# A new order of the work up to block 8, and the keys' maximum spread by a transpose, in a fused attention, feed-forward and soft-MoE kernel

## Chip, cores and metric

The kernel runs on one core of a Trainium2 chip. The metric is the time of one execution on the device, in microseconds (us). The engines' names are those of the profile: PE is TensorE with its matmuls, PEld its loading of weights, DVE VectorE, ACT ScalarE, POOL GpSimd, SP SyncE, which here only issues transfers.

## The reference

Three layers follow each other: a linear attention, a gated feed-forward layer, and a soft mixture of experts.

```python
# attention: B, H, S, D = 8, 8, 576, 64
q_s = exp(q - max(q, -1));  q_s = q_s / (sum(q_s, -1) + 1e-9)
k_s = exp(k - max(k, 2));   k_s = k_s / (sum(k_s, 2) + 1e-9)      # along the sequence
kv  = einsum('bhsd,bhse->bhde', k_s, v)
x   = einsum('bhsd,bhde->bhse', q_s, kv)      # then laid out as x[4608, 512]
# feed-forward: 512 -> 1536 -> 512
x = (silu(x @ w_gate) * (x @ w_val)) @ w_out
# soft MoE: 8 experts with 4 slots each, phi[512, 32], w1[8, 512, 1024], w2[8, 1024, 512]
logits = x @ phi
d = softmax(logits, 0);  slot_input = d.T @ x
slot_out[e] = relu(slot_input[e] @ w1[e]) @ w2[e]
out = softmax(logits, 1) @ slot_out
```

## The kernel before

**Tiles and blocks.** The 4608 tokens are worked on in ten blocks, numbers 0 to 7 of 512 tokens and 8 and 9 of 256. Each array of float64 weights comes in as pairs of 32-bit integers and is made float32 by ACT, DVE and POOL (`cv_a`, `cv_b`, `cv_c`, L513 to L540).

**Attention.** `load_kn`, `load_vn` and `load_q` (L287 to L313) fetch keys, values and queries of one batch (or block) and part. For the keys, `k_max` (L318) takes the maximum over five of a partition's elements on DVE, transposes the 128x128 result on PE (`kpT`, L323) and takes the maximum again on DVE. That leaves one maximum for each of 128 channels, a column of 128x1. `k_exp` (L329) spreads it along the other axis on PE (`kmbp`, L331), subtracts it on DVE and applies the exponential on ACT. `kv` (L340) multiplies keys and values on tiles of 128x32 of the array, 20 small products in all, and DVE and ACT normalise the result into `kvs`. The queries go through `q_a` and `q_b` (L370 to L419). Their transpose `qT` (L442) runs on PE for blocks 0 and 1 and on DVE from block 2 on. `x_mul` (L455) multiplies queries by `kvs` on tiles of 64x64 (`px`, L485). ACT copies `px` to the high half `x` (L495), and DVE subtracts to get the low half (L497).

**Feed-forward.** `pair(n, i)` makes the hidden tile `hT` number i of twelve in block n: a run of twelve products on the full array for the gate (`g`, L595), a run of twelve for the value (`v`, L595), then silu on ACT (L602), a product on DVE (L604). Twelve are four k tiles by three products of halves (weights' high by x high and low, weights' low by x high). The tile of the weights that belongs to i is `W[i]`; its high half is a copy on ACT (L553), its low half a subtraction on DVE. In blocks 0 and 1 each hT goes to memory by a DMA on SP (`hT_dr`, L608), from a pool of six buffers; from block 2 on DVE transposes it (`hB`, L615) and a DMA lays it out anew (L635). In the last blocks PE does that (`hNp`, L641).

**Soft MoE.** `lg` (L661) multiplies hT by `wp`, which is the output weights times phi, on tiles of 128x32. `post_a` to `post_d` form the softmax pieces, and `dh` (L784) gathers the slots' inputs, again on 128x32. After the last block the experts' weights come in 64 pieces (`piece`, L818, on POOL), and the experts and the output follow.

**What sets the order.** All stages are generators. A table of text, `PROGRAM` (L49), lists 2301 steps such as `kexp 0 1` or `pair 3 7`, and each entry moves its generator to its next `yield` (L1109 to L1115). So each engine has its instructions in the order of the table, and nothing else orders them; waits between engines come from what reads and writes what. An entry with `@` makes a POOL instruction wait for a DVE instruction named behind it. The line of k_exp that the change touches is the matmul in

```python
mx, mb = kmax.pop((b, p)), misc((128, 128), "kmbp")
nc.tensor.matmul(mb, lhsT=mx.to_broadcast([128, 128]), rhs=ident, start=True, stop=True)
yield
```

A column repeated 128 times is multiplied by the identity; in the trace this takes two instructions on PE, the transpose `kpT` of the same shape takes one. PSUM tiles for `kpT`, `kmbp`, `kv`, `qT` and `px` come from a pool of three (`misc`), for g and v from two each.

Of the kernel before, what the change touches and what calls it, by code (L numbers as in the profile page):

```python
# [39 lines left out]
def rows(n):  # L40
# [19 lines left out]
    pair 0 0, qb 1 1, wb 1, wb 1, wh 2, pair 0 0, qb 1 1, wb 4, wa 4 2, wl 2 v, wh 3, wb 4, pair 0 2, wa 6 4, wl 3 v,  # L60
    qt 1 0, kmax 1 0, wc 1@wl 3 v, wa 7 5, kmax 1 0, pair 0 2, pair 0 2, kmax 1 1, kmax 1 0, qa 1 2, wh 1, wb 4,
    pair 0 3, pair 0 0, wl 1 v, qb 1 1, pair 0 2, wc 4@wl 1 v, pair 0 0, pair 0 1, pair 0 2, wa 6 4, pair 0 0, wa 5 3,
    wb 6, wb 6, wh 4, kmax 1 1, kexp 1 0, pair 0 1, wb 6, pair 0 1, kexp 1 0, wc 6@wb 6, wa 5 3, kmax 1 1, kexp 1 0,
    pair 0 3, pair 0 1, pair 0 1, wl 4 v, qb 1 2, wb 5, kexp 1 1, kv 1 0, wb 7, qt 1 1, kexp 1 1, kn 1 2, vn 1 3,
    pair 0 4, wh 6, kv 1 0, q 1 3, wb 7, kexp 1 1, wl 6 v, wa 7 5, const rep, wb 5, pair 0 4, kv 1 0, pair 0 4, wb 5,
    kmax 1 2, wc 5@wb 5, pair 0 3, kv 1 1, pair 0 4, qt 1 1, kmax 1 2, pair 0 6, kn 1 3, wa 8 4, pair 0 3, pair 0 4,
    wb 7, vn 1 2, wh 5, pair 0 3, qb 1 2, wa 8 4, wl 5 v, pair 0 6, qb 1 2, wb 8, w 10 1, wb 8, kmax 1 3, wc 7@wb 8,
    pair 0 6, pair 0 5, kv 1 1, kmax 1 2, kv 1 1, pair 0 6, pair 0 6, qa 1 3, wh 7, pair 0 5, wb 8, pair 0 5, qb 1 3,
    wl 7 v, wc 8@wl 7 v, kmax 1 3, kexp 1 2, pair 0 7, pair 0 5, kexp 1 2, pair 0 5, kmax 1 3, wa 9 5, qb 1 3,
    pair 0 7, wh 8, wb 9, wb 9, kexp 1 2, wl 8 v, wa 9 5, kexp 1 3, kv 1 2, wa 10 4, kexp 1 3, pair 0 8, vn 2 0, wb 9,  # L70
    kn 2 1, wa 10 4, kv 1 2, wc 9@wb 9, kexp 1 3, kv 1 2, kv 1 3, pair 0 7, pair 0 8, kv 1 3, wb 10, vn 2 1, w 11 0,
    kn 2 0, wh 9, wb 10, wb 10, kv 1 3, qb 1 3, x 1 0, wl 9 v, pair 0 7, wc 10@wl 9 v, pair 0 8, pair 0 9, x 1 0,
    pair 0 7, pair 0 8, x 1 0, pair 0 8, x 1 0, wh 10, o 1, x 1 0, pair 0 9, pair 0 9, wl 10 v, wa 11 5, kmax 2 0,
    wa 11 5, wb 11, x 1 1, wb 11, wb 11, qt 1 2, x 1 1, pair 0 10, qt 1 2, q 2 1, x 1 1, pair 0 9, wc 11@wb 11, x 1 1,
    x 1 1, pair 0 9, x 1 2, wh 11, o 0, qt 1 3, x 1 2, pair 0 10, wl 11 v, pair 0 10, q 2 3, qt 1 3, qa 2 1, oa 1,
    x 1 2, qa 2 1@wl 11 v, oa 1, x 1 3, pair 0 10, ob 1, pair 0 10, x 1 2, pair 0 11, qa 2 1, x 1 2, qa 2 1@qa 2 1,
    oa 0, ob 1, x 1 3, qb 2 1, x 1 3, pair 0 11, ob 1, ob 0, x 1 3, pair 0 11, x 1 3, oc 1@ob 0, qb 2 1, pair 1 1,
    qa 2 3, oa 0, pair 0 11, qa 2 3, o 3, pair 0 11, ob 0, pair 1 3, ob 0, qa 2 3, oc 0@qa 2 3, pair 1 1, pair 1 1,
    qb 2 1, o 2, qa 2 3, pair 1 0, pair 1 1, qb 2 1, pair 1 1, qb 2 3, qb 2 1@qb 2 1, pair 1 0, qt 2 1, pair 1 0,
    qb 2 3, q 2 0, qb 2 3, pair 1 3, pair 1 3, qb 2 3, pair 1 0, qb 2 3@qb 2 3, pair 1 0, kmax 2 0, op 0, pair 1 3,  # L80
    pair 1 2, oa 2, qa 2 0, pair 1 3, op 0, qa 2 0, oa 2, kmax 2 0, kmax 2 1, ob 2, pair 1 6, ob 2, ob 2, qa 2 0,
    oc 2@qa 2 0, pair 1 2, pair 1 2, qa 2 0, o 4, pair 1 9, pair 1 2, qb 2 0, pair 1 2, qb 2 0, pair 1 9, pair 1 9,
    qb 2 0, qb 2 0, qb 2 0@qb 2 0, kexp 2 0, kmax 2 1, pair 1 4, pair 1 9, kmax 2 1, pair 1 9, qt 2 0, kexp 2 0,
    q 2 2, kexp 2 0, pair 1 6, pair 1 6, pair 1 4, pair 1 4, pair 1 6, qa 2 2, pair 1 6, qa 2 2, pair 1 11, pair 1 4,
    pair 1 4, qa 2 2, qa 2 2@qa 2 2, qb 2 2, kexp 2 1, kv 2 0, kexp 2 1, pair 1 11, vn 2 2, kv 2 0, kn 2 3, kexp 2 1,
    qb 2 2, kv 2 0, qb 2 2, pair 1 11, kv 2 1, qb 2 2, pair 1 10, kv 2 1, vn 2 3, pair 1 11, kv 2 1, kn 2 2,
    qb 2 2@qb 2 2, pair 1 11, kmax 2 3, pair 1 5, kmax 2 3, op 0, op 1, kmax 2 3, op 0, kmax 2 2, kexp 2 3, pair 1 5,
    pair 1 5, kexp 2 3, oa 3, op 1, oa 3, ob 3, ob 3, pair 1 7, kexp 2 3, ob 3, pair 1 5, oc 3@ob 3, pair 1 5,
    kmax 2 2, x 2 0, kmax 2 2, kexp 2 2, pair 1 7, pair 1 7, qt 2 2, o 5, kexp 2 2, q 3 0, qt 2 3, kexp 2 2, q 3 1,
    pair 1 8, pair 1 7, pair 1 7, x 2 0, x 2 0, x 2 0, x 2 0, kv 2 2, kv 2 3, kv 2 2, vn 3 2, kv 2 2, pair 1 8,  # L90
    kn 3 2, pair 1 8, kv 2 3, vn 3 0, qa 3 0, kn 3 0, qa 3 1, qa 3 0, kv 2 3, qa 3 1, x 2 1, pair 1 8, qa 3 0,
    pair 1 8, qa 3 1, op 3, qa 3 0@qa 3 1, x 2 1, pair 1 10, pair 1 10, x 2 1, qa 3 1, x 2 1, kmax 3 2, oa 5, x 2 1,
    qb 3 0, ob 5, pair 2 2, u 0, pair 1 10, ob 5, pair 1 10, oa 5, qb 3 0, qb 3 0@ob 5, pair 2 2, qb 3 1, pair 2 2,
    qb 3 1, qb 3 0, ob 5, op 2, pair 2 2, qb 3 1@ob 5, ua 0, op 1, pair 2 6, op 2, oc 5, op 1, oa 4, oa 4, pair 2 3,
    ob 4, ua 0, qb 3 1, ob 4, ob 4, kmax 3 2, op 2, pair 2 3, pair 2 3, kmax 3 2, qb 3 1@ob 4, op 2, op 3, kmax 3 0,
    oc 4, qt 3 1, pair 2 1, pair 2 3, qb 3 0, ub 0, q 3 3, ub 0, pair 2 1, pair 2 1, ub 0, qt 3 0, uc 0@ub 0,
    pair 2 0, pair 2 1, qa 3 3, q 3 2, ud 0, u 1, qa 3 3, pair 2 0, pair 2 0, qa 3 3, qa 3 3@qa 3 3, qb 3 3, pair 2 4,
    pair 2 0, pair 2 0, pair 2 1, qa 3 2, pair 2 4, pair 2 2, pair 2 4, qa 3 2, qb 3 3, qa 3 2, qb 3 3@qa 3 2, ua 1,
    pair 2 6, qa 3 2, pair 2 4, ua 1, ub 1, ub 1, pair 2 6, ub 1, qb 3 2, pair 2 5, pair 2 6, uc 1, qb 3 2, op 3,
# [1087 lines left out]
```

## Time and profile before

| | before |
|---|---|
| median of three runs | 838.16 us (838.03 to 841.31) |
| profiled execution | 836.75 us, span 835.0 us, 1.75 us around the span |
| mean granted clock of TensorE | 0.99 of full speed |
| PE, DVE, ACT, POOL busy | 789.7, 466.3, 389.3, 259.5 us |
| read and written in HBM | 105.22 MB and 25.17 MB |

The page sums up one profiled execution. Its first part gives busy time by engine, its second part cuts the span into 40 slices of 20.9 us, its fifth part groups instructions by line. Start times of single instructions come from timelines of one engine. A timeline's bar ends where the hardware's pipeline is modelled to end, and so bars of neighbouring products overlap: the distance between two starts says how long the engine was held.

### The profile page before, as it was taken

The numbers are of one execution on the slowest core, as the hardware profiler recorded it, in microseconds if no ns is written. First come the engines' busy times: TensorE is split into PE (matmuls) and PEld (weight loads), VectorE is DVE, ScalarE is ACT, GpSimd is POOL, SyncE is SP. The second block draws the span as 40 slices with busy tenths as digits, with TensorE's granted clock in tenths as the row PEclk, the third lists the DMA queues.
The fourth block names the chain that finished last, engine by engine and source line by source line (L and its number), as shares of the span: only waits on it lengthen the run. The fifth ranks groups of instructions, "written<-read, shape, count | busy, mean of one in ns | idle before, by whom it ended". The sixth has DMA issues, their size and how long they took to land.

```text
span 835.0 us, 15748 instructions
## 1 busy us (share of the span) xinstructions
PE 789.7 (95%) x6045; PEld 603.7 (72%) x6045; DVE 466.3 (56%) x1016; ACT 389.3 (47%) x628; POOL 259.5 (31%) x505
## 2 busy tenths in 40 slices
...
GB/s 346 411 73 177 203 173 143 126 158 96 97 89 158 128 173 160 162 146 183 125 146 141 87 180 183 188 38 117 129 99 105 54 70 296 269 366 392 408 287 355
DMA packets 103243, 151.10 MB, mean 181 GB/s; under 512 B 60032, under 2 KB 73728, under 8 KB 99200
## 3 DMA queue, kind: packets, MB, share of 16 engines
...
q14 instruction: 27, 0.22, 0.1%
HBM read 105.22 MB, written 25.17 MB: 156 GB/s over the span
## 4 chain that ended last, share of the span: by engine, by line
PE 81%; DMA 10%; SPq 3%; DVE 2%; issue 1%; ACT 1%; POOL 0%; DVEq 0%; POOLq 0%
PE v L595 33%; PE g L595 32%; DMA piece<-in_w_dram 3%; PE dh L784 3%; SPq L635 3%; PE lg L661 3%; PE kv L346 2%; PE px L485 2%; DMA f<-in_wgv_dram 2%; DMA vn<-in_vn_dram 1%; PE o L1060 1%; DMA kn<-in_kn_dram 1%; DMA wo<-wo_st 1%; DMA h0T<-hT_dr 1%; PE kmbp L331 1%
## 5 line engine op out<-in xcount | busy, mean ns | idle before, releaser
L595 PE MATMUL g<-x,W 128*128 128x512 f32 (+1 forms) x1440 | 319.5, 373 | 0.0
L595 PE MATMUL v<-x,W 128*128 128x512 f32 (+1 forms) x1440 | 316.7, 371 | 0.0
L595 PEld LDWEIGHTS g<-x,W 128*128 128x128 f32 x1440 | 250.0, 189 | 53.5 <-issue 7.8
L595 PEld LDWEIGHTS v<-x,W 128*128 128x128 f32 x1440 | 249.6, 189 | 51.6 <-issue 7.2
L604 DVE TENSOR_TENSOR hT<-hT,v 128x512 f32<-128x512 f32 (+1 forms) x120 | 75.6, 633 | 162.9 <-PE v L595 126.7
L602 ACT ACTIVATE hT<-g 128x512 f32<-128x512 f32 (+1 forms) x120 | 65.4, 555 | 169.2 <-PE g L595 128.4
L363 POOL COPY qsd<-qsd 32x16 f32<-32x16 f32 (+1 forms) x256 | 52.3, 204 | 111.6 <-DVE qsd L386 61.8
L368 POOL TENSOR_TENSOR qd<-qd,qsd 128x512 f32<-128x512 f32 (+1 forms) x64 | 59.5, 939 | 43.0 <-DVE qsd L390 10.0
L602 ACT ACT_TABLE_LOAD x52 | 66.7, 1283 | 9.5 <-PE g L595 4.0
L615 DVE STREAM_TRANSPOSE hB<-hT 128x512 f32<-128x512 f32 (+1 forms) x78 | 49.8, 670 | 7.7 <-DMA hN<-hB 6.5
L818 POOL DMA_DIRECT2D piece<-in_w_dram x54 | 28.5, 530 | 45.5 <-PE v L595 24.1
L338 ACT ACTIVATE kn<-kn 128x640 f32<-128x640 f32 x32 | 23.4, 737 | 33.9 <-DVE kn L334 31.6
L300 POOL DMA_DIRECT2D vn<-in_vn_dram x24 | 13.5, 562 | 81.1 <-PE kv L346 81.1
...
L495 ACT ACTIVATE x<-px 128x512 fp32r<-128x512 f32 (+1 forms) x44 | 21.2, 514 | 33.8 <-PE px L485 33.7
L540 POOL TENSOR_TENSOR ost<-ost,f 128x1024 int32<-128x1024 int32 x9 | 21.9, 2435 | 38.6 <-DVE W L557 11.7
L334 DVE TENSOR_TENSOR kn<-kn,kmbp 128x640 f32<-128x640 f32 x32 | 25.6, 809 | 13.2 <-PE kmbp L331 13.0
L346 PEld LDWEIGHTS kv<-vn,kn 128*32 128x32 f32 x1280 | 24.5, 149 | 10.2 <-issue 7.0
L419 ACT ACTIVATE qd<-qd 128x512 f32<-128x512 f32 (+1 forms) x32 | 18.0, 576 | 25.7 <-POOL qd L368 25.6
L346 PE MATMUL kv<-vn,kn 128*32 128x65 f32 x1280 | 27.6, 239 | 1.5 <-DMA vn<-in_vn_dram 1.4
L497 DVE TENSOR_TENSOR x<-px,x 128x512 fp32r<-128x512 f32 (+1 forms) x44 | 24.5, 584 | 7.4 <-ACT x L495 7.2
L320 DVE TENSOR_REDUCE kpart<-kn 128x128 f32<-128x640 f32 x32 | 25.9, 808 | 4.9 <-PE kpT L323 2.5
...
## 6 DMA issues: line engine op xcount, KB each, us to landing
...
f<-in_wgv_dram SPq DMA_DIRECT2D x9, 1024.0 KB, 11.0
...
out_dram<-ob SPq DMA_DIRECT2D x7, 1024.0 KB, 10.4
hT_dr<-hT SPq DMA_DIRECT2D x24, 256.0 KB, 3.1
ost<-in_woT_dram SPq DMA_DIRECT2D x6, 1024.0 KB, 6.7
```

What stands on the lines that cost most here:

```text
L320: nc.vector.tensor_reduce(out=part, in_=kn_t[b, p], axis=AX, op=ALU.max)
L334: nc.vector.tensor_tensor(out=t, in0=t, in1=mb.unsqueeze(2).to_broadcast([128, 128, ST]), op=ALU.subtract)
L346: nc.tensor.matmul(acc[r:r + 32, :], lhsT=ek[:, r:r + 32, i], rhs=vv[:, i, r // D, :], start=(i == 0), stop=(i == ST - 1), tile_position=( ...
L363: nc.gpsimd.tensor_copy(out=st[a:a + 32, o + 1], in_=st[b:b + 32, o])
L368: nc.gpsimd.tensor_tensor(out=a, in0=a, in1=s, op=op)
L595: nc.tensor.matmul(gv[j], lhsT=W[i][:, w, k, j, :], rhs=x[:, k, :], start=(k == 0 and w == 0 and x is xh), stop=(k == KT - 1 and w == 1),)
L602: nc.scalar.activation(out=s, in_=g, func=ACTF.Silu)
L604: nc.vector.tensor_tensor(out=s, in0=s, in1=v, op=ALU.mult)
L615: nc.vector.transpose(out=hB[n, i // w][:, :, i % w, :], in_=s.rearrange("p (b j) -> p b j", j=32))
L635: nc.sync.dma_start(out=hN[n][32 * b:32 * b + 32, :, a, w * g:w * g + w, :], in_=src[:, :, b])
L661: nc.tensor.matmul(lg[n][32 * g:32 * g + 32, :], lhsT=wp[:, i, :], rhs=hs[:, g] if n < NSP else hs[g], start=(r == 0), stop=(r == end), ti ...
L818: nc.gpsimd.dma_start(out=ap, in_=src)
```

## The change

Two things change. In `k_exp` the matmul with the identity becomes a transpose of the same repeated column:

```diff
     def k_exp(b, p):
         mx, mb = kmax.pop((b, p)), misc((128, 128), "kmbp")
-        nc.tensor.matmul(mb, lhsT=mx.to_broadcast([128, 128]), rhs=ident, start=True, stop=True)
+        nc.tensor.transpose(mb, mx.to_broadcast([128, 128]), ident)
         yield
 PROGRAM = """
-    q 0 0, q 0 1, const ident, kn 0 1, q 0 3, kn 0 0, w 0, kn 0 2, kn 0 3, q 0 2, w 2, qa 0 0, w 3, w 1, qa 0 1,
+    q 0 0, kn 0 1, qa 0 0, kmax 0 1, q 0 3, qa 0 0, qb 0 0, q 0 1, const ident, qa 0 3, qa 0 1, kmax 0 1, kmax 0 1,
...
```

And the table has the same 2301 steps in another order. The last 396 steps, from the first pieces of the experts' weights on, stand as before. Three places show what the new order does. A row of these listings is a line of code, the instruction, what it writes and reads, its tile, and how often it stands in a row.

PE from the fourth `kmbp` (before) or the third (after) to the first feed-forward product. Before:

```order
L331 MATMUL kmbp<-ident,kmax 128x128
L346 MATMUL kv<-vn_132,kn 32x65 x20
L346 MATMUL kv<-vn,kn 32x65 x20
L346 MATMUL kv<-vn_132,kn_106 32x65 x40
L442 MATMUL qT<-ident,q_95 128x128 x4
L485 MATMUL px<-qsT_184,kvs_91 64x128 x32
L442 MATMUL qT<-ident,q 128x128 x4
L595 MATMUL g<-x_380,W 128x512
```

And now:

```order
L331 MATMUL kmbp<-ident,kmax 128x128
L346 MATMUL kv<-vn_189,kn 32x65 x20
L331 MATMUL kmbp<-ident,kmax 128x128
L346 MATMUL kv<-vn_189,kn_129 32x65 x20
L346 MATMUL kv<-vn,kn 32x65 x20
L346 MATMUL kv<-vn_189,kn_129 32x65 x20
L442 MATMUL qT<-ident,q_95 128x128 x4
L485 MATMUL px<-qsT_155,kvs_91 64x128 x32
L595 MATMUL g<-x_353,W 128x512
```

The second `qT`, which is of block 1, moved behind the first feed-forward product, and the first `kv` moved ahead of the last `kmbp`. On SP, the loads at the start before (`f` are weights as integers, `vn` the values):

```order
L313 DMA q_95<-in_q_dram 128x512
L510 DMA f_110<-in_wgv_dram 128x2048
L510 DMA f_114<-in_wgv_dram 128x2048
L510 DMA f_116<-in_wgv_dram 128x2048
L313 DMA q<-in_q_dram 128x512
L300 DMA vn<-in_vn_dram 128x650
L313 DMA q<-in_q_dram 128x512
L300 DMA vn_132<-in_vn_dram 128x650 x2
L300 DMA vn<-in_vn_dram 128x650
L300 DMA vn_132<-in_vn_dram 128x650
```

And now:

```order
L313 DMA q_95<-in_q_dram 128x512
L510 DMA f_141<-in_wgv_dram 128x2048
L510 DMA f_143<-in_wgv_dram 128x2048
L300 DMA vn_189<-in_vn_dram 128x650
L313 DMA q<-in_q_dram 128x512
L300 DMA vn_189<-in_vn_dram 128x650 x2
L300 DMA vn<-in_vn_dram 128x650
L510 DMA f_243<-in_wgv_dram 128x2048
```

One weight load moved from ahead of the first block's four `vn` to behind them. In the middle, PE around the `kv` and `px` of block 3, before:

```order
L595 MATMUL g<-x_1718,W 128x512
L595 MATMUL g<-x_1717,W 128x512
L485 MATMUL px<-qsT,kvs_91 64x192 x4
L485 MATMUL px<-qsT,kvs_92 64x320 x4
L346 MATMUL kv<-vn,kn 32x65 x20
L661 MATMUL lg<-hT,wp 32x512 x4
L595 MATMUL v<-x_1717,W 128x512
L595 MATMUL v<-x_1718,W 128x512
```

And now:

```order
L595 MATMUL g<-x_1652,W 128x512
L595 MATMUL g<-x_1651,W 128x512
L346 MATMUL kv<-vn,kn 32x65 x40
L661 MATMUL lg<-hT,wp 32x512 x4
L485 MATMUL px<-qsT,kvs_91 64x192 x4
L485 MATMUL px<-qsT,kvs_92 64x320 x4
L595 MATMUL v<-x_1651,W 128x512
L595 MATMUL v<-x_1652,W 128x512
```

Two `kv`, an `lg` and a `px` now stand together between two runs on the full array, where one of the two `kv` stood elsewhere before. Last, SP's writes of hT in block 0 and 1, between loads of weights (`ost` are the output weights as integers), before:

```order
L510 DMA ost<-in_woT_dram 128x2048
L608 DMA hT_dr<-hT 128x512
L510 DMA ost<-in_woT_dram 128x2048
L608 DMA hT_dr<-hT 128x512
L510 DMA ost<-in_woT_dram 128x2048
L608 DMA hT_dr<-hT 128x512
L510 DMA ost<-in_woT_dram 128x2048
L608 DMA hT_dr<-hT 128x512 x3
L510 DMA ost<-in_woT_dram 128x2048
L608 DMA hT_dr<-hT 128x512 x6
```

And now:

```order
L510 DMA ost<-in_wgv_dram 128x2048 x2
L608 DMA hT_dr<-hT 128x512 x2
L912 DMA phi_sb<-in_phi_dram 128x128
L510 DMA ost<-in_woT_dram 128x2048 x2
L608 DMA hT_dr<-hT 128x512 x4
L510 DMA ost<-in_woT_dram 128x2048 x2
L608 DMA hT_dr<-hT 128x512 x6
L510 DMA ost<-in_woT_dram 128x2048
L608 DMA hT_dr<-hT 128x512 x3
```

Loads that stood one by one now stand in twos, and more writes stand in a row behind them.

## Rows read from the trace of the kernel before

**Rows 1.** Page, parts 1 and 2: busy us (share), instructions; GB/s in 40 slices.

```profile
PE 789.7 (95%) x6045; PEld 603.7 (72%) x6045; DVE 466.3 (56%) x1016; ACT 389.3 (47%) x628; POOL 259.5 (31%) x505
...
GB/s 346 411 73 177 203 173 143 126 158 96 97 89 158 128 173 160 162 146 183 125 146 141 87 180 183 188 38 117 129 99 105 54 70 296 269 366 392 408 287 355
```

**Rows 2.** Windows: stretch, length, busy us of PE PEld DVE ACT POOL, clock, DMA, GB/s.

```profile
40.00:60.00 20.00, 19.84 (x89) 15.72 (x88) 18.06 (x24) 19.94 (x42) 7.50 (x4) 1.00 0.25 97
650.00:700.00 50.00, 49.36 (x327) 41.02 (x329) 28.48 (x70) 20.41 (x31) 14.30 (x39) 1.00 0.41 100
800.00:835.00 35.00, 15.93 (x168) 8.58 (x160) 11.67 (x22) 11.59 (x25) 0.00 (x0) 0.80 0.75 304
```

**Rows 3.** Timeline of PE, middle: start us, length us, instructions [idle before <-releaser].

```profile
293.69 0.38 PE L331 MATMUL kmbp<-ident,kmax 128*128 128x128 f32 x2
293.83 3.01 PE L595 MATMUL v<-x,W 128*128 128x512 f32 x12
296.77 0.86 PE L346 MATMUL kv<-vn,kn 128*32 128x65 f32 x40
...
309.78 3.01 PE L595 MATMUL g<-x,W 128*128 128x512 f32 x12
312.72 1.06 PE L661 MATMUL lg<-hT,wp 128*32 128x512 f32 x8
313.71 0.49 PE L331 MATMUL kmbp<-ident,kmax 128*128 128x128 f32 x2
...
477.20 1.04 PE L661 MATMUL lg<-h0T,wp 128*32 128x512 f32 x8
478.06 1.04 PE L661 MATMUL lg<-hT,wp 128*32 128x512 f32 x8
...
486.66 2.88 PE L595 MATMUL v<-x,W 128*128 128x512 f32 x12
489.38 0.27 PE L323 MATMUL kpT<-ident,kpart 128*128 128x128 f32 x1
489.41 3.00 PE L595 MATMUL g<-x,W 128*128 128x512 f32 x12
492.25 2.88 PE L595 MATMUL v<-x,W 128*128 128x512 f32 x12
```

**Rows 4.** Timeline of PE, the start and the first hNp of block 8.

```profile
23.96 4.89 PE L346 MATMUL kv<-vn,kn 128*32 128x65 f32 x160 [1.43 <-DMA vn<-in_vn_dram]
28.78 0.83 PE L442 MATMUL qT<-ident,q 128*128 128x128 f32 x4
...
35.23 0.81 PE L442 MATMUL qT<-ident,q 128*128 128x128 f32 x2 [2.76 <-ACT q L413]
...
36.79 4.22 PE L595 MATMUL g<-x,W 128*128 128x512 f32 x12
...
707.76 0.60 PE L641 MATMUL hNp<-ident,hT 128*128 128x128 f32 x4
```

**Rows 5.** Chain of waits, start of the span: start us, length us, what.

```profile
12.70 11.12 DMA vn<-in_vn_dram
```

**Rows 6.** Timeline of ACT, columns as for PE: copy and conversion of weights.

```profile
26.00 1.05 ACT L553 ACTIVATE W<-ost 128x1024 fp32r<-128x1024 f32 x1
...
38.12 1.18 ACT L518 ACTIVATE ost<-f 128x1024 f32<-128x1024 f32 x1
```

**Rows 7.** Page, part 6: DMA issues, count, KB each, median us to landing.

```profile
f<-in_wgv_dram SPq DMA_DIRECT2D x9, 1024.0 KB, 11.0
...
hT_dr<-hT SPq DMA_DIRECT2D x24, 256.0 KB, 3.1
```

**Rows 8.** Timeline of POOL: two pieces of the experts' weights.

```profile
718.04 1.08 POOL L818 DMA_DIRECT2D piece<-in_w_dram  x2 [6.96 <-PE v L595]
```

**Rows 9.** Page, part 5: line, group, count, busy us, mean ns, idle before.

```profile
L602 ACT ACT_TABLE_LOAD x52 | 66.7, 1283 | 9.5 <-PE g L595 4.0
...
L602 ACT ACTIVATE hT<-g 128x512 f32<-128x512 f32 (+1 forms) x120 | 65.4, 555 | 169.2 <-PE g L595 128.4
```

More of the change, by code (lines that the diff above doesn't have):

```diff
@@ L60 @@
[L60 to L99, printed above, removed]
@@ new lines @@
+    x 2 0, x 2 0, kexp 2 2, kexp 2 2, pair 1 4, qa 2 2@qa 2 2, qb 2 2, qb 2 2, qb 2 2, o 5, pair 1 7, qb 2 3,
+    pair 1 7, x 2 0, x 2 0, qb 2 3@qb 2 3, pair 1 6, kexp 2 3, qb 2 2, qt 2 3, pair 1 11, pair 1 7, pair 1 7,
+    kexp 2 2, pair 1 7, x 2 0, pair 1 10, qb 2 2@qb 2 2, pair 1 6, kv 2 2, qt 2 2, pair 1 6, vn 2 3, q 3 0, kv 2 2,
+    pair 1 0, kv 2 3, op 3, q 3 1, kv 2 3, kn 3 0, qa 3 1, vn 3 0, kv 2 2, op 1, op 1, pair 1 10, pair 1 10, qa 3 1,
+    qa 3 0, qa 3 1, oa 5, kv 2 3, x 2 1, x 2 1, pair 1 10, pair 1 8, x 2 1, ob 5, op 2, x 2 1, qa 3 0, qa 3 0, x 2 1,
@@ new lines @@
+    ub 1, ub 1, ub 1, kn 3 1, qb 3 2, qb 3 2, pair 2 4, pair 2 7, kmax 3 1, kmax 3 1, pair 2 8, kmax 3 1, kexp 3 1,
+    kv 3 0, kexp 3 1, vn 3 3, uc 1, pair 2 8, kexp 3 3, kexp 3 3, pair 2 5, pair 2 9, qb 3 3, pair 2 7, qb 3 2,
+    kv 3 2, kexp 3 1, sh 2 0, sh 2 0, qb 3 2, kexp 3 3, kv 3 1, kv 3 3, ud 1, sh 2 1, sh 2 1, pair 2 7, lg 2 1,
+    kv 3 1, vn 4 1, kv 3 1, x 3 0, x 3 0, pair 2 8, x 3 0, qb 3 2, pair 2 9, qb 3 3, qt 3 3, pair 2 11, q 4 2,
+    pair 2 11, pair 2 9, pair 2 9, qt 3 2, sh 2 1, x 3 0, kv 3 3, kv 3 3, qa 4 2, x 3 1, x 3 1, x 3 0, vn 4 0, op 5,
@@ new lines @@
+    pair 2 10, pair 2 10, x 3 1, x 3 1, kn 4 0, pair 2 11, pair 2 11, op 5, q 4 0, sh 2 1, qa 4 2, qa 4 2, pair 2 11,
+    pair 2 10, x 3 1, kn 4 3, kmax 4 0, pair 3 3, qa 4 0, pair 2 9, qa 4 0, qa 4 0, qa 4 0, qb 4 0, pair 2 10,
+    pair 2 10, pair 3 3, u 2, pair 2 7, ua 2, sh 2 3, pair 2 8, lg 2 2, kmax 4 0, pair 3 6, pair 2 6, pair 3 6,
+    qb 4 0, pa 2, qb 4 0, kmax 4 0, kmax 4 3, ub 2, ua 2, ub 2, kexp 4 0, ub 2, kmax 4 3, pa 2, pb 2, sh 2 3,
+    pair 3 3, qb 4 0, pair 3 3, sh 2 2, pair 3 0, pair 3 6, pair 3 0, kmax 4 3, kexp 4 0, kexp 4 0, pb 2, pair 3 0,
@@ new lines @@
+    pair 3 10, pair 3 5, uc 2, sh 2 2, qa 4 2, pb 2, kv 4 0, ud 2, pair 3 6, kexp 4 3, lt 0 0, pair 3 5, qb 4 0,
+    qt 4 0, q 4 1, ts 0 0, qa 4 1, pair 3 5, pair 3 0, sh 2 3, sh 2 3, ts 0 0, sh 2 2, ts 0 0, kn 4 1, qa 4 1, qa 4 1,
+    qa 4 1, qb 4 1, pb 2, pb 2, kv 4 0, ts 0 0, pair 3 1, pair 3 1, pair 3 1, pair 3 1, qb 4 2, pair 3 1, pair 3 2,
+    sh 2 2, qb 4 1, pair 3 2, kexp 4 3, qb 4 1, qb 4 1, kmax 4 1, pair 3 2, qb 4 2, pair 3 2, ts 0 0, kmax 4 1,
+    kmax 4 1, pair 3 7, vn 4 3, qb 4 1, ts 0 0, kexp 4 1, lg 3 0, lg 0 0, kexp 4 1, kexp 4 1, qb 4 2, qt 4 1,
@@ new lines @@
+    pair 3 8, pair 3 8, kexp 4 2, kexp 4 2, pair 3 7, sh 3 1, pair 3 11, q 5 0, qb 4 3, qt 4 3, kexp 4 2, kv 4 2,
+    kv 4 3, lg 3 1, pair 3 8, pair 3 6, sh 3 1, kv 4 2, kn 5 1, kv 4 2, kv 4 3, kv 4 3, sh 3 2, q 5 1, x 4 1, qa 5 0,
+    x 4 1, x 4 1, x 4 1, sh 3 2, x 4 1, qa 5 0, pair 3 11, pd 2, vn 5 1, pair 3 9, qa 5 0, pair 3 9, kmax 5 1,
+    kmax 5 1, qa 5 0, vn 5 0, pair 4 5, kn 5 0, kmax 5 1, qb 5 0, lt 0 2, pair 3 11, kexp 5 1, qa 5 1, kexp 5 1,
+    pair 3 9, qa 5 1, pair 4 5, qa 5 1, sh 3 2, kmax 5 0, pair 4 4, qb 5 0, sh 3 2, qa 5 1, pair 3 9, pair 4 4,
@@ new lines @@
+    sh 3 3, q 5 3, pair 4 1, pd 2, pb 3, qa 5 3, qa 5 3, pair 4 1, pair 4 1, pb 3, pb 3, sh 3 3, qa 5 3, pb 0, pb 3,
+    pair 4 10, pb 3, pair 4 2, pair 4 2, pair 4 4, sh 3 3, qa 5 3, pb 3, ln 0 0, pair 4 10, pair 4 6, pair 4 2,
+    pair 4 2, kv 5 0, kv 5 0, pair 4 0, ln 0 1, pc 3, pb 0, pc 0, pc 0, pair 4 1, vn 5 2, pd 2, lg 4 0, kmax 5 2,
+    kv 5 0, kn 5 3, vn 5 3, kmax 5 2, pair 4 6, pair 4 6, pair 4 6, kmax 5 3, qb 5 3, qb 5 3, qb 5 3, pair 4 7,
+    kmax 5 2, pair 4 7, kmax 5 3, qa 5 2, sh 4 0, pair 4 7, qb 5 3, ln 0 3, ln 0 2, pair 4 7, pc 0, pc 0, qb 5 2,
```

274 lines of the change are left out of this document (142 added, 132 removed).

## Prediction

> **What bounds the kernel now.** I read the page first: TensorE (PE) is busy for 789.7 of 835.0 us [rows 1]. Then the stretches: from 40 to 760 us PE has almost no idle time; three stretches of 50 us lose 0.34 to 0.64 us each, together 1.5 us, and the last of them stands for the three [rows 2]. The rest of the 45 us of idle time lies before the first feed-forward product at 36.79 us [rows 4] and in the last 75 us, where the experts' weights and the output stream [rows 2]. So the middle is a sum of PE's work, and what an edit there is worth is read from where the next PE row *starts*, not from the length of a bar. Last I read the timeline of PE: a run of twelve products on the full array takes 2.72 us from its start to the start of what follows (486.66 to 489.38 [rows 3]); around products on tiles of the array it takes longer.
>
> **The change part by part: fewer visits to the tiles.** Call it a visit when PE goes from products on the full array to products on tiles (128x32: kv, lg, dh, wpT; 64x64: px) and back. One visit by its rows: the run 309.78 to 312.72, with tiles on both sides, takes 2.94 instead of 2.72 us, 0.22 more (0.09 of it before a tile product, as the run 293.83 to 296.77 shows: 2.94 with a kmbp ahead of it and a tile product behind; the other 0.13 after one). An lg alone on its visit takes 0.99 us (312.72 to 313.71), an lg that is followed by another tile product 0.86 (477.20 to 478.06), so 0.13 more are lost at leaving. A visit costs 0.09 + 0.13 + 0.13, about 0.36 us with rounding [rows 3]. In PE's order between the first feed-forward product and the first hNp I count 63 steps from full array to tiles before, 40 after: 23 x 0.36 = 8.3 us saved (bounds 0.30 to 0.40 each: 6.9 to 9.2). In return px now stands in the same visit as kv and lg: changes between the two tilings go from 7 to 11. No row shows such a change alone; it has no full-array product at either side, so it lies between nothing and a whole visit; I take the part lost at leaving, 0.13, as the nearest: 4 x 0.13 = 0.5 us back (0 to 1.4). Also 8 fewer transposes stand at the edge of a visit, where they share its cost; a lone one costs 0.15 (next paragraph), one at an edge can cost nothing of its own or the same, I take 0.05 each: 0.4 us back (0 to 1.2).
>
> **The transposed maximum.** kmbp is a product in two instructions. Alone between full-array runs it holds PE from 293.69 to 293.83, 0.14, and the run behind takes 2.94, of which 0.09 belongs to the tiles that follow: 0.13 more; together 0.27. The nearest row for the new form is kpT, the same shape as a transpose in one instruction: 489.38 to 489.41, 0.03, and the run behind ends at 492.25, 2.84, 0.12 more; together 0.15 [rows 3]. 0.12 saved, 28 times behind the first product: 3.4 us (bounds 0 and 0.14 each, 3.9). The four ahead of it wait for other engines and are taken at nothing: the loads of the start cover them. The Trainium skill, page "TensorE: Matmul & The Clock Gate", section Part 4: PE-mode transpose, puts a transpose in a kernel at about 275 ns. The trace's bar for kpT is 0.27 us and agrees; the next product, 0.03 us after its start, does not wait for the bar; by the page's figure as a cost this term would be nothing.
>
> **The start.** Before, the first kv product starts at 23.96 us, when vn has landed after 11.12 us in flight [rows 4, 5]; the four kv steps end at 28.78, 1.2 us each; and the first feed-forward product starts at 36.79, 8.0 us later. In SP's new order vn leaves earlier: the load of weights w 1 (1024 KB) and the second block's q now come behind it. Up to that vn the list held 7626 KB (w 1024 by [rows 7]; kn 320, vn 325, q 256 and ident 64 as in the code); the last vn that the four kv steps need now stands at 6996 KB, 630 KB less. At the rate at which the queue moved around there (346 to 411 GB/s, the first two slices of the last line of [rows 1]) that is 1.6 to 1.9 us: it lands at about 22.1, two kv steps of 1.2 us come behind it, so they end at 24.5. Of the 8.0 us behind, 2.76 us idle and the qT of the second block (35.23 to 36.79, 1.56) go, since that qT now stands behind the first product. But ScalarE's new order has a conversion step of w 1 (L518, 1.18) and a copy of weights (L553, 1.05) ahead of the copies that the first px steps wait for [rows 6], and w 1 lands at 8020 KB, some 24.9, 0.4 later than the kv end: 8.0 - 4.3 + 2.2 + 0.4 = 6.3. First product at 30.8, **6.0 us earlier** (bounds: 2, if only the removed waits less the two steps are won; 8, if the two steps hide). From there PE wants a new weight tile each 5.44 us while ScalarE was busy 19.94 of 20 us between 40 and 60 [rows 2]: an earlier PE meets an engine with no room, and I take 1.0 of the 6.0 as given back. The qT that moved behind the first product is now paid there: 0.4.
>
> **What else moves.** ScalarE gets more table loads: by the new order of its activations 113 where the old has 105, 8 more of 1.28 us [rows 9], 10 us on an engine that is busy 47% of the span [rows 1]; PE's slack of one pair hides them, and bare they would cost up to 10. Idle time of PE in the middle (1.5 us) I take as unchanged: its places go, others come. The tail keeps its order, and its loads of weights wait for PE (a row of such, 6.96 us [rows 8]), so it shifts as a whole; the output at the end too.
>
> **Sum.** -8.3 + 0.5 + 0.4 - 3.4 - 6.0 + 1.0 + 0.4 = -15.4 us. The profiled execution took 836.75 us (span 835.0 and 1.75 around it), 1.4 below the median of 838.16: 821.4 against it, **822.8** against the median.
>
> **Rivals.** (a) *Waits inside the visits.* Four visits now hold kv, kv, lg and then the px that reads what kv has just made, through VectorE and ScalarE; before, a run of 2.72 us or more stood between. The cover is one lg, 0.86. If ScalarE is then in a table load and an activation (1.28 + 0.56 [rows 9]), PE waits up to 1.8 each, 7.4 us in all: 830.2. For it speaks the order; against it that ScalarE is busy 47% of the span [rows 1]. The Trainium skill's "TensorEngine Tiling (Array Packing)", Performance Considerations, PSUM Bottleneck, says that tiling speeds up TensorE but not the emptying of PSUM, which is this rival's case; no row of before shows it bind. (b) *The transpose holds PE for its bar.* Then the 28 win nothing: 826.2. Against it the 0.03 above. (c) *The other side: no free hT tile.* Blocks 0 and 1 write 24 tiles hT out over SP, from six buffers. In SP's new order up to six of these writes stand in a row behind one or two loads of weights that wait for GpSimd. A silu that finds no free tile waits for a write, 3.1 us to landing [rows 7], ScalarE stops behind it, and PE two runs later. It decides from five such full waits (15.5 us); with eight the time is 822.8 + 24.8 = 847.6. Against it: such runs stood in the order before as well, six behind one load, without a wait of PE. (d) *The start wins only 2 us and (a) holds:* 822.8 + 4 + 7.4 = 834.2, no change.
>
> **How the numbers follow.** About 0.5% (4.2 us) is what a measurement of this kernel can tell from no change. Forecast as summed, between 816 and 829: 0.73. (a) 0.10, (b) 0.05, (d) 0.07, (c) 0.05. Faster by over 0.5% (below 834.0): 0.73 + 0.10 + 0.05 = 0.88; within: 0.07; slower: 0.05. Low end: visits -9.2, transposes -3.9, start -8.0, idle time -1.5, with 1.3 back: -21.3, near 817, and 816 with the rounding of the start. High end: visits -6.9, transposes -3.4, start -2 and 1.3 back, half of (a): 831. The range 816 to 831 leaves out (c), (d) and the worst of (a).
>
> **What would show it.** The first feed-forward product near 31 us; no qT of the second block ahead of it; kmbp in one instruction with the next start 0.03 us behind; the stretch from the first feed-forward product to the first hNp (36.79 to 707.76 before [rows 4], 671 us) some 9 to 10 us shorter; PE idle in the middle still about 1.5 us; the tail from the first hNp to the end as long as before. I am wrong if the middle shows new idle time at px or dh (a), if silus wait for the hT write (c), or if the first product stays behind 34 us.

## The result, and the profile after

The changed kernel takes 829.52 us (median of six, 827.08 to 832.27) where the kernel before takes 838.50 (six, 837.58 to 841.31): a ratio of 0.9888 (95% interval 0.9868 to 0.9909), 9.0 us faster. Forecast were 15.7 us faster, 822.8 in a range of 816 to 831. So the sign and the range held, and nearly 7 us of the gain are missing. The two profiled executions lie closer together than the medians, 5.2 us by their spans (829.8 against 835.0), so in the traces about 10 us of the forecast gain are missing. This section says where they are.

The profiled execution took 831.53 us, its span 829.8. The page's part 1 (answers to [rows 1]):

```profile
PE 781.6 (94%) x6013; PEld 603.9 (73%) x6013; DVE 481.7 (58%) x1016; ACT 398.8 (48%) x636; POOL 261.7 (32%) x505
```

And two windows with the columns of [rows 2], the second one the stretch from the first feed-forward product to the first hNp:

```profile
40.00:60.00 20.00, 18.96 (x86) 14.91 (x84) 19.90 (x24) 15.46 (x27) 7.43 (x3) 1.00 0.43 152
...
33.38:704.09 670.71, 661.97 (x4560) 514.98 (x4561) 416.92 (x855) 344.19 (x516) 215.17 (x430) 0.99 0.49 140
```

The same stretch of the kernel before, 36.79 to 707.76 [rows 4]:

```profile
36.79:707.76 670.97, 669.33 (x4585) 514.06 (x4586) 403.34 (x851) 333.47 (x501) 214.51 (x431) 1.00 0.48 139
```

PE is busy 7.4 us less, but the stretch is as long as before (670.71 against 670.97): its idle time went from 1.6 us to 8.7. VectorE (the third of the five busy times) is busy 13.6 us more, with almost the same number of operations (855 against 851), and between 40 and 60 us it has 0.1 us to spare, where before it was ScalarE that was full [rows 2]. The timeline of PE (columns of [rows 3]) shows the waits:

```profile
33.38 4.60 PE L595 MATMUL g<-x,W 128*128 128x512 f32 x12 [2.10 <-DVE x L497]
37.82 2.91 PE L595 MATMUL v<-x,W 128*128 128x512 f32 x12
...
61.34 2.57 PE L595 MATMUL g<-x,W 128*128 128x512 f32 x10 [1.61 <-DVE W L557]
...
77.87 4.15 PE L595 MATMUL g<-x,W 128*128 128x512 f32 x10 [1.75 <-DVE W L557]
81.85 2.91 PE L595 MATMUL v<-x,W 128*128 128x512 f32 x12
...
187.77 1.09 PE L485 MATMUL px<-qsT,kvs 64*64 64x128 f32 x16 [2.05 <-DVE wp L580]
...
704.09 0.60 PE L641 MATMUL hNp<-ident,hT 128*128 128x128 f32 x4
```

The first product starts 3.4 us earlier (33.38 against 36.79), and waits 2.10 us for VectorE's subtraction that makes the low half of x (L497). Twice PE waits inside a run for the low half of a weight tile (L557). Behind the first of these waits, ten products take 2.41 us (61.34 to the next start at 63.75). Behind the second they take 3.98 us (77.87 to 81.85), 1.7 more than ten of twelve in 2.72, since the granted clock is lower there (the number ahead of the DMA share: 0.58 and 0.56 of full speed, as means over both of its levels, 1.2 and 2.4 GHz):

```profile
76.00:78.00 2.00, 0.25 (x2) 0.13 (x2) 1.97 (x3) 1.06 (x1) 0.72 (x1) 1.00 0.40 153
78.00:80.00 2.00, 2.00 (x6) 1.56 (x7) 2.00 (x4) 1.77 (x8) 0.10 (x1) 0.58 0.55 119
80.00:82.00 2.00, 2.00 (x7) 1.58 (x6) 1.20 (x2) 2.00 (x4) 2.00 (x1) 0.56 0.96 401
82.00:84.00 2.00, 2.00 (x11) 1.62 (x10) 1.97 (x3) 1.99 (x4) 0.33 (x1) 1.00 0.01 4
```

Why L557 is late stands in the timelines of VectorE and GpSimd, here put side by side, first DVE, then POOL:

```profile
29.45 3.27 DVE L557 TENSOR_TENSOR W<-ost,W 128x1024 fp32r<-128x1024 f32 x1 [0.33 <-ACT W L553]
...
53.43 1.97 DVE L377 TENSOR_SCALAR qst<-qst 128x8 f32<-128x8 f32 x1
...
57.85 3.43 DVE L557 TENSOR_TENSOR W<-ost,W 128x1024 fp32r<-128x1024 f32 x1
```

```profile
29.25 2.39 POOL L540 TENSOR_TENSOR ost<-ost,f 128x1024 int32<-128x1024 int32 x1 [3.42 <-DVE ost L532]
...
52.94 2.44 POOL L540 TENSOR_TENSOR ost<-ost,f 128x1024 int32<-128x1024 int32 x1 [5.49 <-DVE ost L532]
57.46 2.74 POOL L540 TENSOR_TENSOR ost<-ost,f 128x1024 int32<-128x1024 int32 x1 [2.08 <-DVE ost L532]
```

L557 begins at 29.45, 0.2 us behind GpSimd's addition of a weight tile (L540), which ends at 31.64, and ends at 32.72: the addition's end and 1.1 us. L377, an operation on 128x8 that takes 0.17 us, takes 1.97 and ends with the addition at 55.4. By groups up to 100 us, mean ns after the comma, first the changed kernel, then the kernel before:

```profile
L557 DVE TENSOR_TENSOR W<-ost,W 128x1024 fp32r<-128x1024 f32 x10 | 20.2, 2023 | 0.3 <-ACT W L553 0.3
...
L377 DVE TENSOR_SCALAR qst<-qst 128x8 f32<-128x8 f32 x4 | 3.6, 897 | 0.1
```

```profile
L557 DVE TENSOR_TENSOR W<-ost,W 128x1024 fp32r<-128x1024 f32 x11 | 13.4, 1218 | 2.0 <-ACT W L553 2.0
...
L377 DVE TENSOR_SCALAR qst<-qst 128x8 f32<-128x8 f32 x4 | 0.7, 172 | 0.1
```

So the **theory** after the result: some operations of VectorE are held up by a GpSimd addition that runs beside them. Which ones can be read off four traces (before, changed, and the two single parts below). Of operations that begin beside L540, and at least 0.3 us ahead of its end, all 9 L557, 10 L525, 6 L528, 2 L532 and 4 L377 lasted to its end and beyond; 10 L320, 10 L326, 6 L334 and 41 L604 took no longer than alone. Held are operations with two operands in SBUF and the tensor_scalar operations on SBUF; not held are reductions and operations with an operand in PSUM. It goes by which of the two begins first. Where an operation of a held kind had begun already, the addition took longer, here 3.43 us instead of 2.44, first DVE, then POOL:

```profile
73.25 1.22 DVE L532 SCALAR_TENSOR_TENSOR ost<-f,ost 128x1024 int32<-128x1024 int32 x1
```

```profile
73.30 3.43 POOL L540 TENSOR_TENSOR ost<-ost,f 128x1024 int32<-128x1024 int32 x1 [1.49 <-DVE ost L528]
```

The Trainium skill, "SBUF — State Buffer", section "SBUF: two separate sides", states such a rule: VectorE and GpSimd share a pair of ports, and of a GpSimd operation that reads SBUF and a VectorE operation with two inputs in SBUF, or in a mode that uses two ports, the one that starts first holds the pair for the whole instruction while the other waits. The trace agrees in both directions, with 3.27 us for an L557 of 1.22 and the 3.43 us above; which operations run in a mode of two ports, no view here shows.

Below, *held time* is the sum, up to 110 us, of what L557, L532, L525, L528, L377 and L408 take beyond 1.22, 1.22, 0.68, 0.69, 0.17 and 0.16 us, where that is over 0.2. It is 2.4 us (2 operations) before and 18.1 us (13) in the changed kernel, since the new order puts held kinds behind the additions where the old one had mostly reductions and operations that read PSUM (L334, L497, L604). About 1.2 us of the 18.1 stand beside other GpSimd operations (L380, L415). *Rival*: VectorE simply has more to do in that stretch, and GpSimd is beside the point.

### The profile page after: what moved, and what is told of

It reads as the page before. It is cut to its first block, busy times and chain, and to the rows that moved or that the text cites. A ratio compares the mean times of both kernels' runs of the same rounds, so it can differ in the third digit from the quotient of the medians.

```text
span 829.8 us, 15642 instructions
## 1 busy us (share of the span) xinstructions
PE 781.6 (94%) x6013; PEld 603.9 (73%) x6013; DVE 481.7 (58%) x1016; ACT 398.8 (48%) x636; POOL 261.7 (32%) x505
## 4 chain that ended last, share of the span: by engine, by line
PE 83%; DVE 6%; DMA 6%; ACT 2%; issue 1%; SPq 0%; POOL 0%; DVEq 0%; ACTq 0%; POOLq 0%
PE g L595 34%; PE v L595 33%; DMA piece<-in_w_dram 3%; PE lg L661 3%; PE dh L784 3%; PE px L485 2%; PE kv L346 2%; DVE W L557 1%; DMA qd<-in_qd_dram 1%; PE o L1060 1%; DMA f<-in_wgv_dram 1%; DVE ost L532 1%; DVE kn L334 1%; DVE ost L525 1%; PE qT L442 1%
## 5 line engine op out<-in xcount | busy, mean ns | idle before, releaser
L604 DVE TENSOR_TENSOR hT<-hT,v 128x512 f32<-128x512 f32 (+1 forms) x120 | 74.6, 625 | 95.2 <-PE v L595 66.7
L334 DVE TENSOR_TENSOR kn<-kn,kmbp 128x640 f32<-128x640 f32 x32 | 25.7, 809 | 20.8 <-PE kmbp L331 20.8
L540 POOL TENSOR_TENSOR ost<-ost,f 128x1024 int32<-128x1024 int32 x9 | 23.2, 2581 | 40.9 <-DVE ost L532 11.0
L292 POOL DMA_DIRECT2D kn<-in_kn_dram x24 | 13.9, 578 | 68.2 <-PE kv L346 57.5
L497 DVE TENSOR_TENSOR x<-px,x 128x512 fp32r<-128x512 f32 (+1 forms) x44 | 24.7, 577 | 13.3 <-ACT x L495 12.1
L326 DVE TENSOR_REDUCE kmax<-kpT 128x1 f32<-128x128 f32 x32 | 9.1, 285 | 40.0 <-PE kpT L323 39.9
L540 POOL TENSOR_TENSOR ost<-ost 128x1024 int32<-128x1024 int32 x9 | 22.9, 2544 | 21.4 <-DVE ost L532 8.9
L320 DVE TENSOR_REDUCE kpart<-kn 128x128 f32<-128x640 f32 x32 | 25.8, 806 | 6.6 <-DMA kn<-in_kn_dram 6.5
```

Source lines behind the costliest of these rows:

```text
L320: nc.vector.tensor_reduce(out=part, in_=kn_t[b, p], axis=AX, op=ALU.max)
L334: nc.vector.tensor_tensor(out=t, in0=t, in1=mb.unsqueeze(2).to_broadcast([128, 128, ST]), op=ALU.subtract)
L540: nc.gpsimd.tensor_tensor(out=d, in0=d, in1=t[:, c, 0], op=ALU.add)
L604: nc.vector.tensor_tensor(out=s, in0=s, in1=v, op=ALU.mult)
```

## The experiments

In every comparison the kernel before ran on the same chip, at 837.8 to 839.1 us. Changed kernels are compared with each other by their medians, some of which come from different chips.

**1. Each part alone.** The order of before with the new line of `k_exp`, and the new order with the old line:

```diff
-        nc.tensor.matmul(mb, lhsT=mx.to_broadcast([128, 128]), rhs=ident, start=True, stop=True)
+        nc.tensor.transpose(mb, mx.to_broadcast([128, 128]), ident)
```

> The kernel before with the transposed maximum alone; the order stays as before. The sum of the prediction has 28 of these behind the first feed-forward product at 0.12 us each: 3.4 us less than before, 835.1 us beside 838.5, and the kmbp row at one instruction with the next start 0.03 us behind it. The rival (the transpose holds PE for its bar) expects no change within 0.5 us.

> The changed kernel with the old matmul in k_exp: the new order alone. If the two parts add up, 829.5 + 3.4 = 832.9 us; if the waits for VectorE between 54 and 78 us hide it there, some 6 of the 28 win nothing and it is 832.2.

Measured: 834.69 us against 838.61, ratio 0.9951 (0.9932 to 0.9971), 3.9 us faster; and 833.99, ratio 0.9945 (0.9926 to 0.9963), 4.5 slower than the changed kernel. PE's busy time in the stretch is 665.74 in the second, 3.8 more than with the transpose. So by the medians the transposes are worth 3.9 to 4.5 us, a little over the 3.4 forecast, and the new order the other 4.6.

The traces say the same of PE's work, once the busy time in the stretch is cleared of what the lower clock cost (half of the busy time that fell in it: 1.3, 3.3, 3.6 and 3.4 us). It is 668.0 us before, 664.5 with the transposes alone, 662.1 with the order alone and 658.6 with both: 3.5 for the transposes in either order, and 5.9 for the order. The profiled execution of the transposes alone, 836.48, was one of the longer of its ten (831.92 to 838.41): its stretch is as long as before (671.21), since idle time (3.4 us) and the lower clock took the gain back. A row of the changed kernel shows the form:

```profile
339.92 0.27 PE L331 MATMUL kmbp<-ident,kmax 128*128 128x128 f32 x1
339.94 2.33 PE L595 MATMUL v<-x,W 128*128 128x512 f32 x9
```

The next product starts 0.02 us behind it, as behind kpT in [rows 3].

**2. A short addition on GpSimd**, in the changed kernel and in the kernel before. It leaves out 960 of the 1024 columns:

```diff
-        nc.gpsimd.tensor_tensor(out=d, in0=d, in1=t[:, c, 0], op=ALU.add)
+        nc.gpsimd.tensor_tensor(out=d[:, 0:64], in0=d[:, 0:64], in1=t[:, 0:64, 0], op=ALU.add)
```

> The changed kernel, with GpSimd's addition (L540) cut from 1024 columns to 64; the other 960 columns of it are left out. Theory, the engines' lock: VectorE's operations with two operands in SBUF, and its tensor_scalar operations, wait until a GpSimd addition of 2.44 us ends when they start beside it; 11 of them lose some 17 us up to 110 us in the changed kernel, against 2 and 2.4 us in the kernel before. It expects L557 back from a mean of 2.0 us to 1.2, the first feed-forward product near 31.3 instead of 33.4, PE idle between 54 and 78 us of under 1 us instead of 5, the clock at full speed around 78 to 82 us, and 821 to 823 us in all. Rival, plain lack of room on VectorE: the new order gives VectorE more work in that stretch, whatever GpSimd does; L557 may get shorter, but PE still waits 3 us or more there and the time stays above 827.

> The kernel before with the same cut of GpSimd's addition, the control: 960 of 1024 columns of it left out. The lock theory expects little, since only 2 operations of VectorE (2.4 us) are held up there and PE did not wait on them: within 1.5 us of before, L557 at 1.22 us as before. If the cut helped by making the chain of each weight tile shorter, and not by the lock, this kernel would gain as much as the changed one, 6 us or more.

Measured: 819.30 us in the changed kernel, 10.2 less than with the whole addition, ratio 0.9765 (0.9744 to 0.9786); 836.95 in the kernel before, 1.7 less, 0.9977 (0.9962 to 0.9992). Held time is 1.4 and 0 us. Of the changed order with the short addition, a row of PE's timeline, the window of its stretch, and the group of L557:

```profile
31.02 3.03 PE L595 MATMUL g<-x,W 128*128 128x512 f32 x12 [0.19 <-DVE x L497]
33.88 2.89 PE L595 MATMUL v<-x,W 128*128 128x512 f32 x12
```

```profile
31.02:691.51 660.49, 657.58 (x4561) 512.98 (x4561) 396.57 (x855) 344.93 (x518) 168.82 (x430) 1.00 0.51 143
```

```profile
L557 DVE TENSOR_TENSOR W<-ost,W 128x1024 fp32r<-128x1024 f32 x12 | 14.6, 1220 | 3.8 <-ACT W L553 3.8
```

The first product is at 31.02, where 30.8 were forecast; the stretch is 660.5 us, 10.5 shorter than before, where 9 to 10 were forecast; its idle time is 2.9 us. The 10.2 us are more than the 6.7 that went missing, so the loss hangs on that one GpSimd operation. This does not yet say whether through the hold or through the chain of a weight tile, which the cut makes 2.2 us shorter too; that the kernel before gains only 1.7 speaks for the hold, but weakly, since PE had only 1.6 us of idle time in its stretch to win back.

**3. Hold without the longer chain.** The short addition, which leaves out 960 columns, and behind it another one whose result nobody reads:

```diff
+        nc.gpsimd.tensor_tensor(out=t[:, 64:1024, 0], in0=t[:, 64:1024, 0], in1=t[:, 64:1024, 1], op=ALU.add)
```

> The changed kernel with GpSimd's addition cut to 64 columns as in the run with the short addition (960 columns of it left out), but with a second GpSimd addition of 960 columns behind it, in place on the integers, whose result nothing reads. So the chain of a weight tile is as short as there, while GpSimd is at work some 2.4 us beside VectorE as in the changed kernel. Lock theory: L557 is held up again (mean 1.7 us or more up to 100 us), the first feed-forward product comes at 32.5 to 33.5 us and PE waits in the stretch from 50 to 80 us again, 826 us or longer. Rival, the shorter chain (2.2 us less between VectorE's last conversion step and the copy L553): as the short run, 819 to 821 us.

Measured: 824.71 us, ratio 0.9826 (0.9800 to 0.9853), between the two expectations: 5.4 us longer than with the short addition alone, 4.8 shorter than the changed kernel. The second addition took 1.79 us, not 2.4, so only 12.2 us were held, 10.9 more than in the short run, against 16.7 more in the changed kernel. Its L557:

```profile
L557 DVE TENSOR_TENSOR W<-ost,W 128x1024 fp32r<-128x1024 f32 x11 | 16.8, 1525 | 0.0
```

The first product came at 31.03, not at the expected 32.5 to 33.5. The first L557 began at 29.15, ahead of the short addition, and took 1.23 us; so it was the addition that waited, 1.27 us instead of 0.33:

```profile
29.28 1.27 POOL L540 TENSOR_TENSOR ost<-ost,f 128x64 int32<-128x64 int32 x1 [3.42 <-ACT W L553]
```

The hold by itself, with nothing waiting for its result, costs 5.4 us, all of it behind the first product (5.1 by the two ratios, each known to about 2 us). If it costs in proportion, 16.7 us of it cost 8.3 of the 10.2, and about 2 are the chain's; that share is worked out, not measured. The second addition also frees its tile later, but up to 110 us no wait of PE behind the first product names a load.

**4. The addition on VectorE**, which can't be held up by itself:

```diff
-        nc.gpsimd.tensor_tensor(out=d, in0=d, in1=t[:, c, 0], op=ALU.add)
+        nc.vector.tensor_tensor(out=d, in0=d, in1=t[:, c, 0], op=ALU.add)
```

> The changed kernel with the addition L540 on VectorE instead of GpSimd, all work kept. VectorE gets 12 such operations up to 110 us, by the row of L532 (two operands, the same size) 1.22 us each, 14.6 us, and loses the 17 us for which it was held up. Lock theory: L557 back at 1.22 us and L377 at 0.17; VectorE's load about as before, the first feed-forward product 1 to 2 us earlier than 33.4 and, since the chain of a weight tile is 1.2 us shorter, 824 to 829 us. Rival, lack of room on VectorE alone: 14.6 us more on a full engine make it 835 or longer.

Measured: 827.58 us, 0.9876 (0.9854 to 0.9898), within the expected 824 to 829 and within 2 us of the changed kernel. The first product is at 31.19 and L557 at 1.22 us, as the theory says; but 14.6 us of new work on VectorE take the place of 16.6 us that were held, and PE is idle 7.8 us in the stretch. So the rival has its part: VectorE's time, spent or held, is what the stretch from 30 to 80 us has too little of.

**5. The additions of the gate and value weights on VectorE, and two entries moved.** `qt 1 0` of the first step behind the next run of products, and `qa 3 1` of the first step behind `op 1`:

```diff
-        nc.gpsimd.tensor_tensor(out=d, in0=d, in1=t[:, c, 0], op=ALU.add)
+        (nc.vector if key[0] == "w" else nc.gpsimd).tensor_tensor(out=d, in0=d, in1=t[:, c, 0], op=ALU.add)
```

> The changed kernel with all work kept and three edits that the traces point to: the addition L540 of the gate and value weights (12 of 24) on VectorE, so that nothing of VectorE is held up by it; the four qT of block 1 one run of twelve products later (with L540 on VectorE PE waited 2.0 us there, and ran 1.7 us longer at the lower clock after it); and the first step of q's part 1 of block 3 behind the wp copy that the px at 187 us waits for (2.1 us in the changed kernel, 2.1 and about 1.8 at the lower clock with all of L540 on VectorE). Lock theory: these add up, 827.6 less 2.0, 1.7, 2.1 and up to 1.8, and up to 2 more since the later additions are off VectorE again: 818 to 823 us. Rival: the waits only move to the next step of the chain on VectorE, 825 or longer.

Measured: 825.75 us, 0.9844 (0.9822 to 0.9865), with all work kept: 3.8 us less than the changed kernel, and faster than the kernel before and the changed one. It is longer than the 818 to 823 expected and lies where the rival put it (825 or longer): L557 took 1.22 us again up to 110 us, yet waits of 0.5 to 1.5 us came back at other places between 36 and 74 us (6.4 us idle in the stretch). The wait at 187 us is gone; it had been an in-order one: VectorE's reduction of a q tile stood waiting for its load, with the wp copy for px behind it.

**6. Other places for the collisions.** 48 entries of the table moved, no instruction changed; and one added wait (`wc 2` becomes `wc 2@x 0 1`).

> The changed kernel with 48 of its 2301 entries moved, all before block 2's first px but one, so that beside a GpSimd addition VectorE has operations that are not held up (maxima, operations that read PSUM); no instruction added, removed or changed, the addition stays on GpSimd. The last of the 48 is the first step of q's part 1 of block 3, behind the wp copy that the px at 187 us waits for. Lock theory: VectorE's held-up time falls from some 17 us to under 10, the first feed-forward product comes 1 to 2 us earlier, PE's idle time between 50 and 80 us falls from 5 us to 2 or 3, and the wait at 187 us (0.9 and 2.1 in two traces) is gone: 822 to 826 us. Rival, lack of room: the same work on VectorE in the same stretch, so no gain beyond the 1 to 2 us at 187: 827 or longer.

> The changed kernel with one wait added: the second GpSimd addition (weight tile 2, at 29.25 us) waits for the last of the four x subtractions, so the first L557 is not held up. Lock theory, for the start: L557 at 1.22 instead of 3.27 us and the first feed-forward product 2.06 us earlier, at 31.0 to 31.5. For the whole: weight tile 2 comes some 3 us later, and other holds take the place, so 827 to 831 us, no gain to speak of; if one collision were all that was lost, 827 or less.

Measured: 830.58 us, 0.9921 (0.9902 to 0.9941), and 832.08, 0.9934 (0.9921 to 0.9946): neither gains on the changed kernel, and the second is longer. For the first, 822 to 826 were expected of the theory and 827 or longer of the rival, and the rival's came. Held time there fell to 11.7 us and the first product came at 32.33, but of the holds that were left two fell close together on VectorE, 3.9 us in sum, and PE waited 3.00 us behind them:

```profile
53.72 2.95 DVE L532 SCALAR_TENSOR_TENSOR ost<-f,ost 128x1024 int32<-128x1024 int32 x1
...
57.19 3.43 DVE L557 TENSOR_TENSOR W<-ost,W 128x1024 fp32r<-128x1024 f32 x1
```

```profile
60.67 2.60 PE L595 MATMUL g<-x,W 128*128 128x512 f32 x10 [3.00 <-DVE W L557]
```

In the second, the first L557 took 1.23 us as expected, but the first product came at 32.07 (31.0 to 31.5 was expected): the px ahead of it ran at a granted clock of 0.50. The added wait put the addition of weight tile 2 from 29.25 to 34.17, and the waits behind grew. So the sum of held time does not set the end. My reading, which no run isolates, is that what is held on the path of the next weight tile does. Getting rid of one hold gained nothing here while the others stood.

**7. The changed kernel again, and with more visits.** In the second, nine steps that stood beside other tile products stand alone, each behind the next run of twelve, as

```diff
-    kv 4 2, kv 4 3, lg 3 1, x 4 1, pair 3 9
+    kv 4 2, kv 4 3, x 4 1, pair 3 9, lg 3 1
```

(other entries between them left out).

> The changed kernel once more, for a second trace and a time beside the two that follow: 827 to 832 us as before. The lock theory expects VectorE's held-up operations at the same places (they follow from the order), so a first feed-forward product between 32 and 34 us and 4 us or more of idle time on PE between 50 and 80 us; if the trace shows none of it, the first trace was a chance and not the order.

> The changed kernel with nine steps (seven lg, one kv, and one lg ahead of a px) moved each behind the next run of twelve products, so that they stand on a visit of their own: 49 visits to the tiles instead of 40, nothing else changed. By the prediction's price of 0.36 us a visit: 9 x 0.36 = 3.2 us longer, in the stretch from the first feed-forward product to the first hNp, beyond its idle time. If a visit cost nothing of its own and the gain were all the transposes', no change.

Measured: 829.23 us for the changed kernel, with the first product at 33.84, 8.2 us idle in the stretch and 19.1 us held, so the first trace was no chance (the wait at 187 us was 0.87 there). With nine more visits 838.59, 1.0003 (0.9987 to 1.0018): 9.4 longer by the medians, 6.8 by the two spans (836.8 and 830.0), not 3.2. The busy time of the stretch grew by 5.7 to 6.0 us, its idle time by 1.4 to 1.9. One place shows why, first the changed kernel's second trace, then the one with more visits:

```profile
342.45 1.46 PE L346 MATMUL kv<-vn,kn 128*32 128x65 f32 x80 [0.26 <-ACT kn L338]
343.73 1.04 PE L661 MATMUL lg<-hT,wp 128*32 128x512 f32 x8
344.70 1.19 PE L485 MATMUL px<-qsT,kvs 64*64 64x256 f32 x16
345.82 0.96 PE L595 MATMUL g<-x,W 128*128 128x512 f32 x3
```

```profile
342.79 0.72 PE L346 MATMUL kv<-vn,kn 128*32 128x65 f32 x34
343.78 1.71 PE L485 MATMUL px<-qsT,kvs 64*64 64x256 f32 x16 [0.27 <-ACT kvs L355]
345.41 0.98 PE L595 MATMUL g<-x,W 128*128 128x512 f32 x3
```

With the lg between kv and px, px waits for nothing and holds PE 1.12 us. Without it px waits 0.27 us at its head and is 0.5 us longer, since its second half waits for the next `kvs` within the bar. Three such places make about 1.5 of the busy time. What is left, 4.2 to 4.5 us for nine visits, is 0.46 to 0.50 each, and 0.67 if the lower clock's share is taken out (1.5 us here, 3.0 to 3.4 in the changed kernel). So an added visit costs more than the 0.36 forecast. The 23 that the change takes away gave less: 5.9 us for the order (experiment 1) and the 1.3 that the prediction gives back are 0.31 each. No single price fits both. And rival (a) of the prediction is real, but the lg covers it.

## Why the prediction was right and wrong

- **Bound, visits and transposes: right in the sum.** With GpSimd's addition out of the way the stretch came 10.5 us shorter, where 9 to 10 were forecast. In the changed kernel itself PE's busy time fell by 7.4; the first run and the run at 77.87 at the lower clock (4.44 us from start to next start, and 1.7 us over) are 2.1 us more of that than before had (4.06 at its first run), so the work fell by 9.5 against 10.4 in the sum. The transposes' term, 3.4, measured 3.5 by PE's work and 3.9 to 4.5 by the medians. The order's terms, 8.3 less 1.3 given back, measured 5.9; how that divides between fewer visits and changes of tiling is open.
- **The start: right up to its end.** The last kv ended at 24.9 (24.5 forecast), and ScalarE's two steps stood behind it as forecast. First product at 30.8 forecast, 33.38 and 33.84 measured, 31.02 without the hold. The first L557 ends that chain (first product <- x L497 <- L557), at 3.27 us and not 1.22.
- **The step that failed:** "Idle time of PE in the middle (1.5 us) I take as unchanged", and with it the 1.0 us given back. Idle time grew by 7.1 us, between 54 and 78 us above all, and at 187 (2.05, for a load and not a hold, experiment 5). So in the traces the stretch came 0.3 us shorter and not 9.4: 9.5 less work, 7.1 more idle time and 2.1 more at the lower clock. I had named an engine without room, ScalarE, and missed that the new order changes how long VectorE's operations last: the sum has no term for VectorE at all. The trace of before had it: an L525 of 0.68 us takes 1.97 beside an addition that ends at 54.08,

```profile
52.66 1.97 DVE L525 TENSOR_SCALAR ost<-ost 128x1024 f32<-128x1024 f32 x1
```

```profile
51.63 2.45 POOL L540 TENSOR_TENSOR ost<-ost,f 128x1024 int32<-128x1024 int32 x1 [2.96 <-DVE W L557]
```

- **The range held by luck.** Its upper end, 831, rests on half of (a) and on a start that wins only 2 us. Neither came; what filled that room was VectorE.
- **Rivals.** (a) binds only where the cover is taken away (experiment 7). (b) is refuted by experiment 1. (c), no free hT tile, did not come: none of PE's waits in blocks 0 and 1 names a silu. (d) did not come either: the start won 3.4 us and px waited for no kvs.
- **The tail** has the same order; from the first hNp to the end of the span it was 1.5 us shorter in this trace (704.09 to 829.8 against 707.76 to 835.0). No run tested why.

Open is how the 10.2 us divide between hold and chain beyond the proportion in experiment 3, and whether an order exists that keeps the addition on GpSimd and gets below 825.
